# Weight conversion from float64: the sign by a Prelu on ScalarE in place of a GpSimd operation

## The chip, the cores and the metric

The kernel runs on one core of a Trainium2 chip, as one program. The metric is the time of one execution on the device in microseconds. Engines are called by name: TensorE (PE in rows; PEld is its weight load), VectorE (DVE), ScalarE (ACT), GpSimd (POOL) and SyncE (SP), which issues the DMAs.

## The reference

Windowed attention on 4 x 8 heads of 576 tokens (four heads with a window of 32, four with a dilated one), then two feed-forward layers on the 2304 tokens. Cut to its core:

```python
attn = softmax(where(mask, q @ k.T / 8, -1e9)) @ v
x = attn_out.transpose(0, 2, 1, 3).reshape(2304, 512)
xn = x / sqrt(mean(x * x) + 1e-6) * rms_g
y = (silu(xn @ w_gate) * (xn @ w_val)) @ w_out            # 512 -> 1536 -> 512
h = y @ w_in                                              # 512 -> 1024
solu = h * softmax(h)
out = (solu - mean(solu)) / sqrt(var(solu) + 1e-6) * g_ln @ w_out2
```

The weight matrices arrive as float64, since the scales that they were multiplied by are float64; q, k, v and the gains are float32.

## The kernel before

**Data.** Every product of a weight is made of three matmuls: the operand and the weight are each split into a high part, rounded to TensorE's float32 format, and the low rest (mm3, lines 607 to 609). The weights come in 52 tiles of 128x512 float64: 36 for the first layer (w1: 12 slices f of the hidden width, each with a tile for gate, value and output) and 16 for the second.

**Conversion.** `prepare` makes each float64 tile into float32 by integer work on its two 32-bit words. A DMA brings the raw tile (`fetch`). `shifted` (line 264) multiplies the high word, read as a float32, by 2^-112 on ScalarE, which moves the exponent's offset from float64's to float32's; the result is tile tf. `signs` (line 272) multiplies the high word by zero on GpSimd, which leaves a zero with the weight's sign in tile wf. `parts` (line 277) shifts the low word right by 29 and ORs it into wf on VectorE. `joined` (line 282) shifts tf left by 3, which drops its sign, and ORs it into wf on VectorE. `scaled` multiplies 8 of the tiles by the gain. `halves` (ScalarE) writes the high part h_w into the raw tile's buffer, and `lows` writes the rest, on GpSimd or VectorE. wf has 4 slots; a tile's slot is free again after its `lows`.

**Stages.** Attention for tokens 0 to 511 comes first, in pieces of 256 tokens, each followed by its root mean square (`rms`: squares, a matmul with ones, `eps`, `root` as a power on GpSimd, `diag` on VectorE, `spread` on TensorE, then scaling, high and low parts of x). The first layer runs over f for a piece of tokens: gate (g), value (vp), tanh, two products on VectorE, high and low parts (uh), output (y). Attention for the later pieces is laid between these products. The 36 tiles of w1 are converted while the first pieces run; the 16 tiles of the second layer are fetched into the buffers of w1 as the last piece lets go of them. The second layer then runs over 18 blocks of 128 tokens (`p_h`, `p_t`, `p_products`).

**Order.** All steps up to the second layer are written to the engines' queues in an order that a planner in the kernel works out (`Plan.order`). Each step has its engine or engines with a cost in us, the steps that it needs, the slots that it takes and a due time. At each turn the engine whose first step can start earliest takes, among the steps that could start within 0.25 us of that, the one with the lowest due time. A step with two engines goes to the one on which it ends first. The due times of w1's tiles are 14 + 2.72 us for each; those of the first attention groups rise by 2.5 us each. While TensorE would idle in the plan before the first `spread`, small dummy matmuls (warm) are written. The queues run in order on the chip, each instruction when its semaphores allow.

Of the kernel before, what the change touches and what calls it, by code (L numbers as in the profile page):

```python
# [7 lines left out]
F32 = mybir.dt.float32  # L8
# [3 lines left out]
U32 = mybir.dt.uint32  # L12
AF = mybir.ActivationFunctionType
ALU = mybir.AluOpType
# [6 lines left out]
P = 128  # L21
# [175 lines left out]
def tile_attention_glu_solu(ctx: ExitStack, tc: tile.TileContext, qk_d, v_d, w1_d, win2_d, wout2_d,  # L197
                            rmsg_d, gln_d, mask_d, ident_d, out):
    nc = tc.nc
    ENG = {"a": nc.scalar, "d": nc.vector, "p": nc.gpsimd}  # L200
    const = ctx.enter_context(tc.tile_pool(name="const", bufs=1))
    wp = ctx.enter_context(tc.tile_pool(name="wp", bufs=1))
    stg = ctx.enter_context(tc.tile_pool(name="stg", bufs=1))
# [24 lines left out]
    plan = Plan({"qk": 2, "v": 2, "a": 2, "y0": 1, "y1": 1, "y2": 1, "y3": 1, "g": 1, "vp": 1, "s": 3, "pT": 2, "x": 1,  # L228
                 "sq": 2, "rs": 1, "u": 2, "uh": 2, "yo": 2, "wf": 4, "bh": 1, "bl": 1, "ch": 1, "cl": 1,
                 "yl": 3, "yh": 3} | {f"w{f}_{i}": 1 for f in range(NF1) for i in range(3)})  # L230
    T = {}

    def new(pool_, key, shape, dtype=F32, name=None):

        tag, i = plan.where[key]
        T[key] = pool_.tile(shape, dtype, tag=f"{tag}{i}", name=name or tag)
        return T[key]

    def put(e, dst, src, scale=None):
        if e == "a":  # L240
            nc.scalar.copy(dst, src) if scale is None else nc.scalar.mul(dst, src, scale)  # L241
        elif e == "p":
            nc.gpsimd.tensor_scalar(dst, src, 1.0 if scale is None else scale, 1.0, ALU.mult, ALU.mult)
        elif scale is None:
            nc.vector.tensor_copy(dst, src)  # L245
        else:
            nc.vector.tensor_scalar(dst, src, scale, None, ALU.mult)

    def less(e, dst, a, b):
        ENG[e].tensor_tensor(dst, a, b, ALU.subtract)  # L250
# [5 lines left out]
    def prepare(key, tag, src, scale, due, needs=()):  # L256
        k, raw, tf, wf, th = ((x, key) for x in ("k", "raw", "tf", "wf", "th"))

        def fetch(e):
            r = T[raw] = wp.tile([P, 512, 2], I32, tag=tag, name=f"raw_{tag}")  # L260
            nc.sync.dma_start(out=r.rearrange("p n t -> p (n t)"), in_=src.bitcast(I32))

        def shifted(e):
            put(e, new(stg, tf, [P, 512], name="tf"), T[raw][:, :, 1].bitcast(F32), 2.0 ** -112)

        def wf_():
            return T["wf", key[0]][:, plan.where[wf][1]]

        def signs(e):
            if ("wf", key[0]) not in T:  # L270
                T["wf", key[0]] = xn.tile([P, 4, 512], F32, tag="cl0", name="wf")
            ENG[e].tensor_scalar(wf_(), T[raw][:, :, 1].bitcast(F32), 0.0, 1.0, ALU.mult, ALU.mult)  # L272

        def parts(e):

            w = wf_().bitcast(U32)
            nc.vector.scalar_tensor_tensor(out=w, in0=T[raw][:, :, 0].bitcast(U32), scalar=29, in1=w,
                                           op0=ALU.logical_shift_right, op1=ALU.bitwise_or)

        def joined(e):  # L280
            w = wf_().bitcast(U32)
            nc.vector.scalar_tensor_tensor(out=w, in0=T[tf].bitcast(U32), scalar=3, in1=w,
                                           op0=ALU.logical_shift_left, op1=ALU.bitwise_or)

        def scaled(e):
            put(e, wf_(), wf_(), scale)

        def halves(e):

            T[th] = wp.tile([P, 2, 512], F32R, tag=tag, name=f"h_{tag}")  # L290
            put(e, T[th][:, 0], wf_())

        def lows(e):
            less(e, T[th][:, 1], wf_(), T[th][:, 0])
            (w1 if key[0] == 1 else w2)[key[1:]] = T[th]

        plan.add((key, "fetch"), {"s": 1.6}, fetch, needs, due=due - 12)
        plan.add((key, "shifted"), {"a": 0.68}, shifted, [(key, "fetch")], takes=[("yo", tf)], due=due)
        lead = (key[0],) + ((0, 0) if key[0] == 1 else (0,))
        plan.add((key, "signs"), {"p": 1.0}, signs, [(key, "fetch")] + [(lead, "signs")] * (key != lead),  # L300
                 takes=[("wf", wf)] + [("cl", ("stage", key[0]))] * (key == lead), uses=[("stage", key[0])], due=due)
        plan.add((key, "parts"), {"d": 0.72}, parts, [(key, "signs")], due=due)
        plan.add((key, "joined"), {"d": 0.72}, joined, [(key, "parts"), (key, "shifted")], uses=[tf], due=due)
        before = "joined"
        if scale is not None:
            plan.add((key, "scaled"), {"d": 0.45, "p": 0.92}, scaled, [(key, "joined")], due=due)
            before = "scaled"
        plan.add((key, "halves"), {"a": 0.62}, halves, [(key, before)], due=due)
        plan.add((key, "lows"), {"p": 1.6, "d": 1.0}, lows, [(key, "halves")], uses=[wf, ("stage", key[0])], due=due)
# [499 lines left out]
    for name, t, src in (("mask", masks_t, mask_d), ("ident", ident, ident_d), ("rmsg", rmsg, rmsg_d), ("gln", gln, gln_d)):  # L809
        plan.add((name,), {"s": 0.5 if name in ("mask", "ident") else 0.1},  # L810
                 lambda e, t=t, src=src: nc.sync.dma_start(out=t, in_=src),
                 due={"mask": -9, "ident": -5.5}.get(name, 3))
# [8 lines left out]
    for f in range(NF1):  # L821
        for i in range(3):
            prepare((1, f, i), f"w{f}_{i}", w1_d[f, :, i * 512:(i + 1) * 512], None, 14 + 2.72 * (3 * f + i))
# [5 lines left out]
    for u in range(16):  # L829
        f, i = u // 3, u % 3  # L830
        src = win2_d[u // 2, :, (u % 2) * 512:(u % 2 + 1) * 512] if u < 8 else wout2_d[u - 8]
        prepare((2, u), f"w{f}_{i}", src, None if u < 8 else gln[:, u - 8:u - 7], 5000 + u,
                [("out", last, f, 1) if i == 2 else (("g", "vp")[i], last, f, 1)] + ([("gln",)] if u >= 8 else []))
# [130 lines left out]
```

## Time and profile before

| what | us |
|---|---|
| median of 3 runs | 790.29 |
| lowest to highest | 788.03 to 791.84 |
| the profiled execution, its own time | 789.12 |
| span of its instructions | 787.3 |
| TensorE busy | 762.3 |
| VectorE busy | 442.3 |
| ScalarE busy | 315.5 |
| GpSimd busy | 162.0 |

The span goes from the first instruction to the last. A busy time is the time in which at least one instruction of the engine ran; matmuls overlap, so a busy TensorE isn't TensorE at its peak. In rows, L272 is line 272 of the kernel, and a tile is named by the kernel's names, out<-in.

### The profile page before, as it was taken

The page shows a single profiled execution, that of the slowest core. Times are in us where ns is not written, and L with a number is a line of the kernel's source. Part 1 is how long each engine was busy: PE and PEld are TensorE (multiplying, and loading weights), DVE is VectorE, ACT ScalarE, POOL GpSimd, SP SyncE. Part 2 cuts the span into 40 slices and gives each one's busy share as a digit, 9 for nine tenths or more (in the row PEclk, how much of TensorE's full clock was granted, in tenths as well). Part 3 has the DMA queues.
Part 4 walks back from the last instruction along what each step waited for, and adds up shares of the span by engine and source line. Part 5 has one row for each costly group of instructions (what it writes and reads, how often), then busy time and mean ns, then how long its engine had stood idle before and what let it go on. Part 6 is the DMA issues. An engine that isn't in the chain of part 4 may idle for free. (4 is left out here: it accounts for less than half of the span.)

```text
span 787.3 us, 12213 instructions
## 1 busy us (share of the span) xinstructions
PE 762.3 (97%) x4776; PEld 627.9 (80%) x4776; DVE 442.3 (56%) x835; ACT 315.5 (40%) x780; POOL 162.0 (21%) x206
## 2 busy tenths in 40 slices
PE   8779999899999999999999999989999999999997
PEld 6668777689997787887788888768878888888886
DVE  4889999965444344434354438982255544444542
ACT  3555666644333333324333325431134434434432
POOL 1333544521120120210110304530011101101100
PEclk9999999999999999999999999999999999999999
DMA  7997111033014101033211027500101111111101
GB/s 258 359 409 297 56 39 72 25 127 124 14 28 137 65 32 48 1 104 120 76 36 49 1 97 235 163 27 1 63 4 54 50 32 54 42 40 54 35 33 41
DMA packets 34233, 68.94 MB, mean 88 GB/s; under 512 B 3328, under 2 KB 13568, under 8 KB 34176
## 3 DMA queue, kind: packets, MB, share of 16 engines
q1 hardware_dynamic: 34176, 68.16, 25.5%
q8 instruction: 38, 0.62, 0.3%
q14 instruction: 19, 0.16, 0.1%
HBM read 58.71 MB, written 9.44 MB: 87 GB/s over the span
## 5 line engine op out<-in xcount | busy, mean ns | idle before, releaser
L607 PE MATMUL y<-uh,h_w 128*128 128x512 f32 (+1 forms) x252 | 93.9, 372 | 1.3 <-ACT uh L241 0.9
L608 PE MATMUL y<-uh,h_w 128*128 128x512 f32 (+1 forms) x252 | 91.0, 361 | 0.8 <-DVE uh L250 0.8
L609 PE MATMUL y<-uh,h_w 128*128 128x512 f32 (+1 forms) x252 | 90.9, 361 | 0.4 <-DVE h_w L250 0.4
L643 DVE SCALAR_TENSOR_TENSOR u<-u,g 128x512 f32<-128x512 f32 (+1 forms) x63 | 38.3, 608 | 87.3 <-ACT u L637 86.9
L607 PE MATMUL vp<-xh,h_w 128*128 128x512 f32 (+1 forms) x204 | 81.4, 399 | 0.6 <-DVE u L647 0.6
L607 PE MATMUL g<-xh,h_w 128*128 128x512 f32 (+1 forms) x204 | 79.8, 391 | 2.1 <-DVE u L643 2.0
L609 PE MATMUL vp<-xh,h_w 128*128 128x512 f32 (+1 forms) x204 | 77.6, 380 | 0.9 <-POOL h_w L250 0.9
L608 PE MATMUL g<-xl,h_w 128*128 128x512 f32 (+1 forms) x204 | 77.5, 380 | 0.8 <-POOL xl L250 0.5
L609 PE MATMUL g<-xh,h_w 128*128 128x512 f32 (+1 forms) x204 | 77.5, 380 | 0.1
L608 PE MATMUL vp<-xl,h_w 128*128 128x512 f32 (+1 forms) x204 | 77.4, 379 | 0.0
L637 ACT ACTIVATE u<-g 128x512 f32<-128x512 f32 (+1 forms) x63 | 33.6, 534 | 79.6 <-PE g L609 79.2
L272 POOL TENSOR_SCALAR wf<-raw_w 128x512 f32<-128x512 f32 x52 | 46.1, 888 | 93.8 <-DVE h_w L250 44.7
L503 POOL TENSOR_TENSOR sq<-x 128x256 f32<-128x256 f32 x30 | 20.0, 669 | 219.5 <-DVE x L245 179.3
L241 ACT CAST uh<-u 128x512 fp32r<-128x512 f32 (+1 forms) x63 | 35.2, 558 | 74.0 <-DVE u L647 74.0
L647 DVE SCALAR_TENSOR_TENSOR u<-u,vp 128x512 f32<-128x512 f32 (+1 forms) x63 | 38.3, 608 | 43.4 <-PE vp L609 43.2
L762 POOL TENSOR_SCALAR st<-st 128x1 f32<-128x1 f32 x18 | 13.5, 748 | 222.8 <-ACT sq L760 222.8
L384 ACT ACTIVATE s<-s,nm 128x64 f32<-128x64 f32 x120 | 40.3, 337 | 45.9 <-DVE nm L370 45.9
L746 PE MATMUL h<-h_w,yh 128*128 128x512 f32 x144 | 58.2, 404 | 0.0
L787 PE MATMUL o<-h_w,lt 128*128 128x512 f32 (+1 forms) x152 | 57.9, 381 | 0.2 <-DVE lt L775 0.2
L785 PE MATMUL o<-h_w,lt 128*128 128x512 f32 (+1 forms) x152 | 57.7, 380 | 0.0
L786 PE MATMUL o<-h_w,lt 128*128 128x512 f32 (+1 forms) x152 | 57.6, 379 | 0.0
L748 PE MATMUL h<-h_w,yh 128*128 128x512 f32 x144 | 57.0, 396 | 0.0
(116 smaller groups left out, 1663.5 us busy)
## 6 DMA issues: line engine op xcount, KB each, us to landing
raw_w<-w SPq DMA_DIRECT2D x36, 512.0 KB, 10.2
vt<-v SPq DMA_DIRECT2D x38, 256.0 KB, 3.0
qk<-qk SPq DMA_DIRECT2D x20, 400.0 KB, 4.0
y<-yT SPq DMA_DIRECT2D x18, 256.0 KB, 3.1
yT<-yo SPq DMA_DIRECT2D x16, 256.0 KB, 2.3
raw_w<-win SPq DMA_DIRECT2D x8, 512.0 KB, 4.6
raw_w<-wout SPq DMA_DIRECT2D x8, 512.0 KB, 4.2
out<-ob SPq DMA_DIRECT2D x16, 256.0 KB, 2.1
```

The lines of the kernel that those rows point to most:

```text
L272: ENG[e].tensor_scalar(wf_(), T[raw][:, :, 1].bitcast(F32), 0.0, 1.0, ALU.mult, ALU.mult)
L384: nc.scalar.activation(T[s_][:, i], (T[sp] if first else T[s_])[:, i], AF.Exp, scale=0.125 if first else 1.0, bias=st["nm"][:, i:i + 1], a ...
L607: nc.tensor.matmul(acc, wh, xh, start=first, stop=False)
L608: nc.tensor.matmul(acc, wh, xl, start=False, stop=False)
L609: nc.tensor.matmul(acc, wl, xh, start=False, stop=last)
L643: return lambda e: nc.vector.scalar_tensor_tensor(out=u_of(f), in0=u_of(f), scalar=1.0, in1=T["g", v, f], op0=ALU.add, op1=ALU.mult)
L647: return lambda e: nc.vector.scalar_tensor_tensor(out=u_of(f), in0=u_of(f), scalar=0.5, in1=T["vp", v, f], op0=ALU.mult, op1=ALU.mult)
L746: nc.tensor.matmul(h[:, n], yh[:, 0, k], w[:, 0], start=(k == 0), stop=False)
L748: nc.tensor.matmul(h[:, n], yh[:, 1, k], w[:, 0], start=False, stop=(k == KD - 1))
L785: nc.tensor.matmul(o, lt[:, 0, k], w[:, 0], start=(k == 0), stop=False)
L786: nc.tensor.matmul(o, lt[:, 0, k], w[:, 1], start=False, stop=False)
L787: nc.tensor.matmul(o, lt[:, 1, k], w[:, 0], start=False, stop=(k == NF2 - 1))
```

## The change

The Prelu in `shifted` scales by 2^-112 and multiplies negative results by -2^32. A negative weight's tf is thus positive and has one exponent bit set that no other weight sets; the shift left by 3 in `joined` moves that bit into the sign's place. `signs` and its step are gone. `parts` writes wf where it had ORed into it, as a one-source shift; it needs only the fetch (and the first tile's `parts`, where it had been the first tile's `signs`), takes the wf slot, and has a cost of 0.42 in the plan where it had 0.72.

```diff
--- before.py
+++ after.py
@@ -261,21 +261,19 @@
             nc.sync.dma_start(out=r.rearrange("p n t -> p (n t)"), in_=src.bitcast(I32))
 
         def shifted(e):
-            put(e, new(stg, tf, [P, 512], name="tf"), T[raw][:, :, 1].bitcast(F32), 2.0 ** -112)
+
+
+            nc.scalar.activation(new(stg, tf, [P, 512], name="tf"), T[raw][:, :, 1].bitcast(F32), AF.Prelu,
+                                 scale=2.0 ** -112, alpha=-2.0 ** 32)
 
         def wf_():
             return T["wf", key[0]][:, plan.where[wf][1]]
 
-        def signs(e):
+        def parts(e):
+
             if ("wf", key[0]) not in T:
                 T["wf", key[0]] = xn.tile([P, 4, 512], F32, tag="cl0", name="wf")
-            ENG[e].tensor_scalar(wf_(), T[raw][:, :, 1].bitcast(F32), 0.0, 1.0, ALU.mult, ALU.mult)
-
-        def parts(e):
-
-            w = wf_().bitcast(U32)
-            nc.vector.scalar_tensor_tensor(out=w, in0=T[raw][:, :, 0].bitcast(U32), scalar=29, in1=w,
-                                           op0=ALU.logical_shift_right, op1=ALU.bitwise_or)
+            nc.vector.tensor_scalar(wf_().bitcast(U32), T[raw][:, :, 0].bitcast(U32), 29, None, ALU.logical_shift_right)
 
         def joined(e):
             w = wf_().bitcast(U32)
@@ -297,9 +295,8 @@
         plan.add((key, "fetch"), {"s": 1.6}, fetch, needs, due=due - 12)
         plan.add((key, "shifted"), {"a": 0.68}, shifted, [(key, "fetch")], takes=[("yo", tf)], due=due)
         lead = (key[0],) + ((0, 0) if key[0] == 1 else (0,))
-        plan.add((key, "signs"), {"p": 1.0}, signs, [(key, "fetch")] + [(lead, "signs")] * (key != lead),
+        plan.add((key, "parts"), {"d": 0.42}, parts, [(key, "fetch")] + [(lead, "parts")] * (key != lead),
                  takes=[("wf", wf)] + [("cl", ("stage", key[0]))] * (key == lead), uses=[("stage", key[0])], due=due)
-        plan.add((key, "parts"), {"d": 0.72}, parts, [(key, "signs")], due=due)
         plan.add((key, "joined"), {"d": 0.72}, joined, [(key, "parts"), (key, "shifted")], uses=[tf], due=due)
         before = "joined"
         if scale is not None:
```

## Rows read from the trace of the kernel before

**Rows 1.** The page, part 1: busy us, share of the span, instructions.

```profile
PE 762.3 (97%) x4776; PEld 627.9 (80%) x4776; DVE 442.3 (56%) x835; ACT 315.5 (40%) x780; POOL 162.0 (21%) x206
```

**Rows 2.** Table by stretches: the stretch, its length, each engine's busy us, TensorE's clock, DMA.

```profile
30.00:70.00 40.00, 32.17 (x278) 28.76 (x277) 36.85 (x76) 20.25 (x50) 12.39 (x15) 0.96 1.03 407
70.00:150.00 80.00, 78.64 (x509) 63.04 (x509) 76.46 (x128) 50.04 (x126) 36.56 (x38) 1.00 0.17 58
150.00:160.00 10.00, 7.80 (x74) 5.48 (x72) 9.79 (x17) 5.68 (x17) 6.05 (x7) 1.00 0.39 136
...
500.00:540.00 40.00, 37.79 (x162) 29.69 (x161) 30.44 (x42) 15.34 (x27) 12.88 (x11) 1.00 0.17 54
```

**Rows 3.** Waits of TensorE, 28 to 70 us: us, times, longest.

```profile
PE pv L419 <- DVE x L245: 2.2, 1, 2.2
PE rs L536 <- DVE rd L533: 1.6, 2, 0.8
PE vp L609 <- POOL h_w L250: 0.9, 1, 0.9
```

**Rows 4.** Waits of TensorE, 70 to 165 us.

```profile
PE tp L402 <- DVE s L396: 1.4, 2, 0.7
PE tp L402 <- DVE x L245: 1.1, 1, 1.1
```

**Rows 5.** Groups by line and shape: count | busy us, mean ns | idle us before.

```profile
L272 POOL TENSOR_SCALAR wf<-raw_w 128x512 f32<-128x512 f32 x52 | 46.1, 888 | 93.8 <-DVE h_w L250 44.7 <-DMA raw_w<-win 26.9 <-DMA raw_w<-w 18.1
...
L241 ACT ACTIVATE tf<-raw_w 128x512 f32<-128x512 f32 x52 | 34.6, 671 | 10.8 <-DVE wf L282 4.7 <-DMA raw_w<-win 3.6 <-DMA raw_w<-w 1.5
...
L637 ACT ACTIVATE u<-g 128x512 f32<-128x512 f32 x45 | 26.8, 595 | 70.8 <-PE g L609 70.8
...
L760 ACT ACTIVATE sq<-e,st 128x1024 f32<-128x1024 f32 x18 | 20.7, 1151 | 35.0 <-DVE st L758 35.0
...
L250 POOL TENSOR_TENSOR h_w<-wf,h_w 128x512 fp32r<-128x512 f32 x14 | 19.1, 1363 | 24.1 <-ACT h_w L241 18.7 <-issue 5.4
...
L247 DVE TENSOR_SCALAR wf<-wf,gln 128x512 f32<-128x512 f32 x4 | 1.9, 483 | 0.1
...
L854 ACT ACT_TABLE_LOAD x1 | 1.3, 1283 | 0.7 <-PEq L957 0.7
```

**Rows 6.** Tile raw_w: ns min/median/max, first and last start in us.

```profile
L272 POOL TENSOR_SCALAR wf<-raw_w x52: 635/974/1181, 12.4 to 517.8; 128x512 f32<-128x512 f32 x52
...
L277 DVE SCALAR_TENSOR_TENSOR wf<-raw_w,wf x52: 674/684/1784, 21.0 to 521.9; 128x512 uint32<-128x512 uint32 x52
```

**Rows 7.** Order of time, GpSimd: start us, us, instruction.

```profile
26.70 1.10 POOL L272 TENSOR_SCALAR wf<-raw_w 128x512 f32<-128x512 f32 x1 [4.49 <-DMA raw_w<-w]
27.77 0.72 POOL L528 TENSOR_TENSOR r<-r,mhalf 128x2 f32<-128x2 f32 x1
...
61.27 1.28 POOL L250 TENSOR_TENSOR h_w<-wf,h_w 128x512 fp32r<-128x512 f32 x1 [1.36 <-ACT h_w L241]
```

**Rows 8.** Order of time, VectorE.

```profile
28.52 0.48 DVE L533 TENSOR_SCALAR rd<-ident,r 128x128 f32<-128x128 f32 x2 [1.24 <-POOL r L528]
...
61.84 1.26 DVE L282 SCALAR_TENSOR_TENSOR wf<-tf,wf 128x512 uint32<-128x512 uint32 x1
```

**Rows 9.** Line 277 (parts) by stretches: VectorE's busy us and count.

```profile
30.00:70.00 40.00, 7.38 (x11) 0.96 1.03 407
70.00:160.00 90.00, 19.90 (x25) 1.00 0.19 67
```

**Rows 10.** Line 272 (signs) by stretches: GpSimd's busy us and count.

```profile
30.00:70.00 40.00, 6.57 (x9) 0.96 1.03 407
70.00:160.00 90.00, 19.87 (x22) 1.00 0.19 67
460.00:540.00 80.00, 15.49 (x16) 1.00 0.40 129
```

**Rows 11.** Waits over the whole span: us, times, longest.

```profile
POOL wf L272 <- DMA raw_w<-w: 18.1, 4, 11.1
```

## Prediction

> **What bounds the kernel now.** I read the busy times first [rows 1]: TensorE is busy for 762.3 of 787.3 us, so all that an edit on the other engines can win is TensorE's 25 us of idle time and whatever makes its own work run late or slowly. The next view is the table by stretches [rows 2], because the average hides where the idle time lies. In 30 to 70 us TensorE is busy for 32.17 of 40 us, and VectorE for 36.85: 7.8 us of TensorE are lost while VectorE is nearly full. In 70 to 150 us TensorE loses 1.4 us and in 150 to 160 us 2.2 us, with VectorE at 76.46 of 80 and 9.79 of 10. In 500 to 540 us it loses 2.2 us, with VectorE at 30.44 of 40. These are just the stretches in which weights are converted: 36 tiles up to 160 us, 16 tiles after 467 us. The waits of TensorE say what ended its idle time there: VectorE's copy into x (2.2 us) and VectorE's diagonal rd (1.6 us) early [rows 3], VectorE's s and x after 70 us [rows 4]. So weight conversion competes with attention and the gated products for VectorE, and VectorE's queue is what TensorE waits for. GpSimd has time left, but it isn't innocent, as the next part shows.
>
> **What goes away: 52 sign operations on GpSimd.** They take 888 ns each, 46.1 us in all [rows 5]; the shortest takes 635 ns [rows 6]. The difference is a collision. In one place GpSimd works on a low half from 61.27 to 62.55 us, and a joining instruction on VectorE that starts at 61.84 us takes 1.26 us [rows 7, 8], where the parts instruction of the same size has a median of 684 ns [rows 6]: it ends about 0.6 us late, roughly what GpSimd still had to do when it began. Seen from GpSimd, the sign operations lose 6.57 - 9 x 0.635 = 0.9 us in 30 to 70 us, 19.87 - 22 x 0.635 = 5.9 us in 70 to 160 us and 15.49 - 16 x 0.635 = 5.3 us in 460 to 540 us [rows 6, 10]. I take as much for what VectorE loses to them, as an estimate: a collision holds up one side or the other. The Trainium skill says the same under GPSIMD Engine Reference, Specifications: GpSimd's SBUF interfaces are shared with VectorE, and it contends with instructions of VectorE that read two SBUF operands or run in a 2-port mode; by that rule the new, one-source parts instruction would still collide with whatever GpSimd work is left, so that the collisions would shrink and not vanish. The trace agrees with the first half; no row of it shows a one-source conversion step beside GpSimd.
>
> A second cost goes with them. GpSimd takes its work in order, and at 26.70 us a sign operation, having waited 4.49 us for its DMA, runs until 27.80 us; the power for the first tile's mean square can start only at 27.77 us, and VectorE's rd idles 1.24 us for it [rows 7, 8]. That chain leads through TensorE's spread and the scaling of x to the first gate matmul, and nothing hides it.
>
> **What is changed on VectorE.** Parts becomes a one-source shift in place of a two-source shift and OR. The nearest row below is the one-source multiplication of a 128x512 tile in SBUF, 483 ns [rows 5]; the nearest above is the parts instruction as it is, 684 ns [rows 6]. I take 483 ns, since it has the same number of operands and the same size. What speaks for the upper end is that the source is read at every second word, but the old parts instruction read it so too. The saving is then 0.20 us a tile; at the upper end it is 0.
>
> **What is changed on ScalarE.** The scaled copy (671 ns) becomes a Prelu with the same source, scale and destination [rows 5]. No row has a Prelu. Nearest below is the tanh of 128x512, 595 ns; the next function above is the square of twice the size, 1151 ns [rows 5]. I take 671 ns, since scaled copy, tanh and square run at nearly the same pace. The bounds are -52 x 0.08 = -4 us and 52 x 0.48 = 25 us of ScalarE's time. It is spread over stretches in which ScalarE is busy for half of the time (20.25 of 40 us, 50.04 of 80 us) [rows 2], and that idle time hides it: I take 0. If the cover were gone at the upper end, 36 x 0.48 = 17 us would fall into the first conversion, with some 50 us of idle time against it, so I leave it out of the range.
>
> **What is moved.** Parts now waits for the DMA itself, where the sign operation had waited (18.1 us in all, four times, for the first weights [rows 11]). Behind it in VectorE's queue stand attention, the norm and the gated products. It costs nothing as long as parts comes up after the landing: the first sign operation starts at 12.4 us, the first parts at 21.0 us [rows 6], and the order is by due time, which the change leaves alone. Behind GpSimd's missing instruction come the power, the squares, the low halves of x and 14 of the 52 low halves of weights; all move up. ScalarE's and SP's steps keep their needs; no DMA is added. The planner lays out the whole order anew with parts at 0.42 for 0.72 and GpSimd free, so single instructions will stand elsewhere.
>
> **The sum.** VectorE is relieved by 11 x 0.20 + 0.9 = 3.1 us in 30 to 70 us and by 25 x 0.20 + 5.9 = 10.9 us in 70 to 160 us [rows 9, 10], and by 16 x 0.20 + 5.3 = 8.5 us in the second conversion. Not all of it is time:
> - up to 30 us: the power comes about 1.2 us earlier, which is on the path: -1.2 us.
> - 30 to 70 us: 3.8 us of the waits are put down to VectorE in [rows 3] alone, 7.8 us are idle, so most of the 3.1 us can be won. I take 70%: -2.2 us.
> - 70 to 160 us: 10.9 us of relief meet 3.6 us of idle TensorE; beyond that TensorE is the limit. I take 40% of the idle time, since part of it ends with ScalarE's or TensorE's own chain: -1.4 us.
> - 500 to 540 us: 2.2 us idle, but there parts follows the landing closely and may wait for it: -0.2 us.
>
> Together -5.0 us. The profiled execution took 789.1 us (span 787.3 us and 1.8 us around it), which makes 784.1 us; it lay 1.2 us under the median of 790.3 us, so the forecast is 785.3 us. The bounds: with no saving on parts and only the earlier power, -1 us; with all idle time of the three stretches and the power won, -(1.2 + 7.8 + 3.6 + 2.2) = -15 us, which I don't believe, as TensorE also waits for DMA and for its own results.
>
> **The rivals.**
> 1. Hidden: TensorE gets its operands no earlier because its own order and ScalarE's chain come last. For it: TensorE is busy for 78.64 of 80 us in the longest conversion stretch. Against: the 7.8 us lost in 30 to 70 us. Time: 789 to 790 us.
> 2. Low halves go to GpSimd (the other side). The planner gives each of the 52 low halves to whichever of VectorE and GpSimd ends first; with GpSimd free, more than the present 14 may go there, at 1363 ns each [rows 5] against 684 ns on VectorE for work of that size [rows 6]. TensorE then waits for them: 0.9 us, the one time it shows [rows 3]. The gain of 5.0 us is eaten by six such waits, and at ten the kernel is 4 us slower: 794 us. Against it: 14 such steps now cause one such wait, so ten would need some 140.
> 3. VectorE blocks on landings: parts planned ahead of the data stops everything behind it. If the 18.1 us of GpSimd's DMA waits [rows 11] fell on VectorE, less the first, in which VectorE has nothing to do anyway (11.1 us), it would be 7 us: 790.3 - 5.0 + 7 = 792 us. Against: the 9 us between the first sign operation and the first parts.
> 4. The change doesn't do what it says: Prelu lies outside the loaded function table. Only one table load stands in the trace, 1283 ns [rows 5], and it serves the exponential, tanh, square and copies. If Prelu needed its own, each of 52 would bring two loads, 104 x 1.28 = 133 us on ScalarE, half of it hidden at best: 857 us or more. The Trainium skill has the rule under ScalarE: Activation LUTs, Table sets: functions are loaded in named sets, a function outside the active set needs a load, and cheap functions such as relu and copy are in every set. By that rule the question is whether Prelu counts as such a filler; no row of this trace shows a Prelu.
>
> **How the numbers follow.** The forecast (781 to 788.5 us as its own range) has a chance of 0.58, rival 1 0.22, rival 2 0.10, rival 3 0.07, rival 4 0.03. A change of 0.5%, 3.95 us, is about what the measurement of this kernel can tell from none: faster means under 786.3 us, slower over 794.2 us. Of the forecast 0.50 lies under 786.3 us and 0.08 above; rival 1 gives 0.02 to faster and 0.20 to same; rival 2 splits in halves, rival 3 gives 0.04 to slower, rival 4 all. Faster 0.52, same 0.36, slower 0.12. The range of 8 in 10 leaves out the far end of rivals 2 to 4 and gains above 10.5 us: 779.8 to 791.8 us.
>
> **What would show it.** GpSimd's busy time falls by about 46 us, unless low halves fill it; parts shows a median near 483 ns; Prelu near 671 ns with one table load in all; rd waits less than 0.3 us for the power and the first gate matmul starts about 1.2 us earlier; TensorE is busy for over 34 us of the 40 that follow 30 us. I'm wrong if TensorE's idle time in 30 to 70 us stays near 7.8 us, if its waits for low halves from GpSimd grow to several us, or if VectorE's parts waits for raw weights.

## The result and the profile after

| what | before | after |
|---|---|---|
| median, us | 790.61 | 781.59 |
| lowest to highest | 788.03 to 791.84 | 779.74 to 783.07 |
| the profiled execution, its own time | 789.12 | 782.46 |
| span of its instructions | 787.3 | 780.7 |

The ratio after to before is 0.9889, with a 95% interval of 0.9854 to 0.9923: 9.0 us less, where 5.0 us had been forecast. The profiled executions differ by 6.7 us alone; before's was 1.5 us under its median, and after's 0.9 us over.

The page of the changed kernel, part 1 (as [rows 1]), and its table by stretches (as [rows 2]):

```profile
PE 763.8 (98%) x4775; PEld 634.7 (81%) x4775; DVE 416.3 (53%) x838; ACT 315.8 (40%) x781; POOL 111.2 (14%) x150
```

```profile
30.00:70.00 40.00, 35.57 (x277) 33.09 (x276) 31.79 (x76) 21.83 (x54) 5.99 (x7) 0.79 0.98 381
70.00:150.00 80.00, 78.53 (x551) 64.44 (x550) 75.12 (x140) 54.45 (x140) 23.37 (x22) 1.00 0.23 80
150.00:160.00 10.00, 10.00 (x71) 7.67 (x70) 3.93 (x9) 2.42 (x7) 2.36 (x4) 1.00 0.38 122
500.00:540.00 40.00, 40.00 (x178) 33.12 (x177) 22.98 (x38) 13.30 (x23) 2.64 (x2) 1.00 0.13 41
```

GpSimd loses 50.8 us of work and VectorE 26.0. The numbers in brackets are counts of instructions, and where the same kind of work runs they say more than TensorE's busy time. In 30 to 70 us TensorE is 3.4 us busier than before, yet ran 277 matmuls where it had run 278: its granted clock was 0.79 there where it had been 0.96. In 70 to 160 us it ran 620 where it had run 581 (the rows count a matmul that crosses their border twice); of these 39, 20 only make up for work that came later (up to 70 us it had run 570 where it had run 590), and the stretch mixes short matmuls of attention with longer ones, so that its count alone doesn't size the gain. In 500 to 540 us all matmuls are of one size. There it ran 178 where it had run 162, and the stretch ahead shows that 178 is what 40 us hold when nothing is late (table by stretches, before):

```profile
460.00:500.00 40.00, 40.00 (x178) 33.12 (x177) 29.32 (x38) 17.12 (x29) 14.18 (x14) 1.00 0.63 203
```

Groups by line and shape, after (as [rows 5]); then tile raw_w (as [rows 6]):

```profile
L280 DVE SCALAR_TENSOR_TENSOR wf<-tf,wf 128x512 uint32<-128x512 uint32 x52 | 37.2, 717 | 3.7 <-ACT tf L266 0.6 <-DVE wf L276 0.5
L266 ACT ACTIVATE tf<-raw_w 128x512 f32<-128x512 f32 x52 | 34.6, 674 | 9.7 <-DMA raw_w<-win 4.7 <-DMA raw_w<-wout 2.6 <-DMA raw_w<-w 2.3
...
L276 DVE TENSOR_SCALAR wf<-raw_w 128x512 uint32<-128x512 uint32 x52 | 25.5, 493 | 1.9 <-DMA raw_w<-win 1.9
```

```profile
L276 DVE TENSOR_SCALAR wf<-raw_w x52: 415/421/1514, 21.2 to 514.4; 128x512 uint32<-128x512 uint32 x52
```

Parts has a median of 421 ns (before 684). The joining step, whose instruction is unchanged, has a mean of 717 ns where it had 862 (the same group of before), which the experiments below put down to GpSimd being out of its way.

Where the 6.6 us of span lie is read from the starts of four kinds of instruction in order of time: the first gate matmul, the first gate matmul of the last pieces (g<-xhl), the first fetch of the second layer's weights (it stands on SP, and waits for buffers to come free), and the first matmul of the second layer. Before:

```profile
31.14 0.39 PE L607 MATMUL g<-xh,h_w 128*128 128x256 f32 x1
...
165.05 0.28 PE L607 MATMUL g<-xhl,h_w 128*128 128x256 f32 x1
...
467.28 3.04 SPq L261 DMA_DIRECT2D raw_w<-win  x2
...
565.94 0.39 PE L746 MATMUL h<-h_w,yh 128*128 128x512 f32 x1
```

After:

```profile
33.50 0.39 PE L604 MATMUL g<-xh,h_w 128*128 128x256 f32 x1
...
163.21 0.28 PE L604 MATMUL g<-xhl,h_w 128*128 128x256 f32 x1
...
464.30 3.03 SPq L261 DMA_DIRECT2D raw_w<-win  x2
...
559.29 0.39 PE L743 MATMUL h<-h_w,yh 128*128 128x512 f32 x1
```

| stage | before, us | after, us | change | forecast |
|---|---|---|---|---|
| to the first gate matmul | 31.14 | 33.50 | +2.4 | -1.2 |
| to g<-xhl (36 tiles converted) | 133.91 | 129.71 | -4.2 | -3.6 |
| to the second layer's first fetch | 302.23 | 301.09 | -1.1 | 0 |
| to the second layer (16 tiles converted) | 98.66 | 94.99 | -3.7 | -0.2 |
| second layer | 221.4 | 221.4 | 0 | 0 |

### The profile page after: what moved, and what is told of

The parts are those of the page before. It is cut to its first block, busy times and chain, and to the rows that moved or that the text cites. A ratio compares the mean times of both kernels' runs of the same rounds, so it can differ in the third digit from the quotient of the medians.

```text
span 780.7 us, 12092 instructions
## 1 busy us (share of the span) xinstructions
PE 763.8 (98%) x4775; PEld 634.7 (81%) x4775; DVE 416.3 (53%) x838; ACT 315.8 (40%) x781; POOL 111.2 (14%) x150
## 4 chain that ended last, share of the span: by engine, by line
PE 89%; DVE 5%; DMA 2%; issue 1%; ACT 1%; POOL 1%; SPq 0%; ACTq 0%; POOLq 0%; DVEq 0%
PE vp L604 7%; PE y L604 6%; PE vp L606 6%; PE vp L605 6%; PE g L604 6%; PE y L605 6%; PE g L606 6%; PE y L606 6%; PE g L605 6%; PE h L745 4%; PE h L743 4%; PE h L744 4%; PE o L784 4%; PE o L783 4%; PE o L782 4%; PE pv L416 3%
## 5 line engine op out<-in xcount | busy, mean ns | idle before, releaser
L743 PE MATMUL h<-h_w,yh 128*128 128x512 f32 x144 | 58.2, 404 | 0.0
L745 PE MATMUL h<-h_w,yh 128*128 128x512 f32 x144 | 57.0, 396 | 0.0
L744 PE MATMUL h<-h_w,yh 128*128 128x512 f32 x144 | 56.8, 395 | 0.0
L604 PEld LDWEIGHTS y<-uh,h_w 128*128 128x128 f32 x252 | 48.0, 191 | 9.1 <-ACT uh L241 1.2
```

The lines of the kernel that those rows point to most:

```text
L604: nc.tensor.matmul(acc, wh, xh, start=first, stop=False)
L743: nc.tensor.matmul(h[:, n], yh[:, 0, k], w[:, 0], start=(k == 0), stop=False)
L744: nc.tensor.matmul(h[:, n], yh[:, 0, k], w[:, 1], start=False, stop=False)
L745: nc.tensor.matmul(h[:, n], yh[:, 1, k], w[:, 0], start=False, stop=(k == KD - 1))
```

## The experiments

Three theories stood against each other. A: the time comes from the operations, that is from VectorE's shorter step and from the collisions that leave with GpSimd's sign operations. B: it comes from the order, which the planner lays out anew with GpSimd free and parts at 0.42. C: it is made or lost ahead of the first gate matmul, and the rest only keeps that lead. Each experiment is an edit of the changed kernel; ratios are to the kernel before, measured beside it on the same chip. None leaves anything out of the computation; e2, e7 and e8 add work on GpSimd whose result nobody reads.

### The changed kernel again, and the new operations in the old order

e0 is the changed kernel. In e1 the planner sees the old steps, so that the work is laid out as before, but the step of the sign operation emits nothing:

```diff
-        plan.add((key, "parts"), {"d": 0.42}, parts, [(key, "fetch")] + [(lead, "parts")] * (key != lead),
+        plan.add((key, "signs"), {"p": 1.0}, lambda e: None, [(key, "fetch")] + [(lead, "signs")] * (key != lead),
...
+        plan.add((key, "parts"), {"d": 0.72}, parts, [(key, "signs")], due=due)
```

> The changed kernel once more, beside the experiments, as their common measure. Theory A (the operations themselves: less GpSimd work that collides with VectorE, a shorter parts) and theory B (the planner's new order) both expect 780 to 783 us against 790.6 us before. By its profile the TensorE clock stood at half speed from 26.5 to 29.9 us and from 36.7 to 53.8 us; if that belongs to this order and is no accident, it shows again here.

> The new operations in the order of the kernel before: the planner still counts a step of 1.0 us on GpSimd and 0.72 us for parts, but the GpSimd step writes no instruction. Queues of TensorE, ScalarE and SP are those of the kernel before, VectorE's differs only in the form of parts. Theory A: all of the gain, 781 to 783 us. Theory B: none of it, 789 to 791 us. A share in between splits the gain between the two.

e0 took 780.57 us, ratio 0.9849 (0.9818 to 0.9881), with 792.77 us before beside it: 12.2 us. e1 took 784.35 us, ratio 0.9894 (0.9858 to 0.993): 8.4 us of the 12.2 are there without the new order. Neither theory had this: A expected 781 to 783 us and B 789 to 791. The two intervals overlap, so that the order's 3.8 us are a difference of medians, and the profiles show little of it: from the first gate matmul to g<-xhl e1 takes 130.2 us, where e0 takes 128.9 and the result's profile 129.7, and the later stages agree to 0.2 us.

### The old operations in the new order

e6 is the other corner: the scaled copy (not shown in the cut), GpSimd's sign operation (emitted inside parts) and the two-source parts, in the plan of the changed kernel.

```diff
...
-            nc.vector.tensor_scalar(wf_().bitcast(U32), T[raw][:, :, 0].bitcast(U32), 29, None, ALU.logical_shift_right)
+            w = wf_().bitcast(U32)
+            nc.gpsimd.tensor_scalar(wf_(), T[raw][:, :, 1].bitcast(F32), 0.0, 1.0, ALU.mult, ALU.mult)
+            nc.vector.scalar_tensor_tensor(out=w, in0=T[raw][:, :, 0].bitcast(U32), scalar=29, in1=w,
+                                           op0=ALU.logical_shift_right, op1=ALU.bitwise_or)
```

> The three old operations (scaled copy, sign on GpSimd, two-source parts that waits for it) in the order of the changed kernel. With the GpSimd work back this order took 791 us, with the two-source parts 785 us, the changed kernel 781 us. Theory A (operations; their costs add up): 793 to 797 us, slower than the kernel before by 1 to 4 us, since this order counts on a short parts and an idle GpSimd. Theory B (the new order is better by itself by some 4 us, as the run with the old order suggests): 787 to 789 us.

It took 808.45 us, ratio 1.0217 (1.0183 to 1.025) to 792.96 us: 15.5 us slower than before, and outside what either theory gave. Waits of VectorE (30 to 165 us) and of TensorE (70 to 165 us) in e6:

```profile
DVE wf L277 <- POOL wf L276: 7.7, 8, 1.8
```

```profile
PE tp L401 <- DVE s L395: 9.3, 5, 3.2
```

The new order puts parts where no sign operation has to be waited for. With one there, VectorE stops for 7.7 us in its queue, and TensorE behind it for 9.3 us. So B falls as a cause by itself: the same order loses 15.5 us with the old operations, while with the new ones its median lies 3.8 us lower. The four corners do not add up, and neither does an account that prices operations and order apart.

### GpSimd's work back, and cut in two

e2 puts a GpSimd operation of nearly the old size back beside each parts, into a tile that nobody reads (`spare`). VectorE doesn't wait for it. But it reads the raw tile, into which `halves` writes, so `halves` waits for it. e8 keeps that wait and takes away the work (one column is read). e7 adds the work back, reading a constant in place of the raw tile.

```diff
 e2:
+            nc.gpsimd.tensor_scalar(spare, T[raw][:, 0:480, 1].bitcast(F32), 0.0, 1.0, ALU.mult, ALU.mult)
 e8:
+            nc.gpsimd.tensor_scalar(spare[:, 0:1], T[raw][:, 0:1, 1].bitcast(F32), 0.0, 1.0, ALU.mult, ALU.mult)
 e7: as e8, and
+            nc.gpsimd.tensor_scalar(spare, mhalf[:, 0:1].to_broadcast([P, 480]), 0.0, 1.0, ALU.mult, ALU.mult)
```

> The changed kernel in its own order, with 52 sign operations back on GpSimd, on 480 of 512 columns, into a spare tile that nobody reads; halves must wait for them before it overwrites the raw tile. Theory A with the collisions as its larger part: 4 to 6 us slower than the changed kernel, 786 to 788 us, with joined and the low halves back near 860 and 760 ns in the mean. Theory A with parts as its larger part, and theory B: within 1 us of the changed kernel.

> The changed kernel in its own order with GpSimd kept as busy as by the sign operations, but with nothing of weight waiting for it: for each tile a one-column read of the raw tile, and then 480 columns read from a constant and written to a spare tile. Theory A with the collisions as the cause: as slow as with the sign operations back, 788 to 792 us. Rival: the cost lay in what waited for the sign operation (halves, which overwrites the raw tile): 780 to 783 us.

> The same with the one-column read alone: the wait of halves for GpSimd is there, GpSimd's long work is not. Theory A with the collisions as the cause: within 2 us of the changed kernel, 780 to 783 us. Rival (the wait): as slow as with the sign operations back, 788 to 792 us.

| kernel | median, us | ratio to before, interval |
|---|---|---|
| e2, work and wait | 791.35 | 0.9996 (0.9968 to 1.0024) |
| e7, work apart and wait | 787.19 | 0.9926 (0.9895 to 0.9958) |
| e8, wait alone | 782.17 | 0.9846 (0.9814 to 0.9878) |
| e0, neither | 780.57 | 0.9849 (0.9818 to 0.9881) |

Groups by line and shape, e2:

```profile
L282 DVE SCALAR_TENSOR_TENSOR wf<-tf,wf 128x512 uint32<-128x512 uint32 x52 | 42.0, 809 | 3.2 <-ACT tf L267 0.3
L277 POOL TENSOR_SCALAR spare<-raw_w 128x480 bf16<-128x480 f32 x52 | 41.4, 797 | 38.3 <-DMA raw_w<-win 31.8 <-DMA raw_w<-wout 4.7
...
L642 DVE SCALAR_TENSOR_TENSOR u<-u,g 128x512 f32<-128x512 f32 x45 | 30.8, 684 | 78.8 <-ACT u L636 78.8
...
L278 DVE TENSOR_SCALAR wf<-raw_w 128x512 uint32<-128x512 uint32 x52 | 28.5, 550 | 1.4 <-DMA raw_w<-win 1.4
```

The same view, e7 and then e8:

```profile
L283 DVE SCALAR_TENSOR_TENSOR wf<-tf,wf 128x512 uint32<-128x512 uint32 x52 | 40.7, 784 | 3.7 <-ACT tf L267 0.6 <-ACT h_w L242 0.5
L278 POOL TENSOR_SCALAR spare<-mhalf 128x480 bf16<-128x480 f32 x52 | 39.7, 763 | 4.3
```

```profile
L282 DVE SCALAR_TENSOR_TENSOR wf<-tf,wf 128x512 uint32<-128x512 uint32 x52 | 37.8, 728 | 3.3 <-ACT tf L267 0.5
...
L277 POOL TENSOR_SCALAR spare<-raw_w 128x1 bf16<-128x1 f32 x52 | 18.7, 359 | 48.3 <-DMA raw_w<-win 35.8 <-DMA raw_w<-wout 10.8
```

Waits of ScalarE's `halves` for the GpSimd operation over the whole span, e7 and then e8:

```profile
ACT h_w L242 <- POOL spare L277: 9.4, 9, 2.5
```

```profile
ACT h_w L242 <- POOL spare L277: 6.1, 4, 2.1
```

e2 gives back all that the change had won: with the shorter parts, the Prelu and the new order in place, 52 unread operations on GpSimd cost 10.8 us. It is not the wait that costs: in e8 ScalarE waits 6.1 us for the short operations, which add 18.7 us to GpSimd's work, and the kernel is as fast as e0, while the same view of e2 has no such wait at all. It is the work on many elements: with it the unchanged joining step takes 809 ns (e2) and 784 ns (e7), without it 728 (e8) and 717 (the changed kernel). The work that e7 adds to e8 shares no tile with VectorE's conversion, so a shared tile isn't needed for the collision.

The traces show the collision directly, instruction by instruction. In the 14 profiles of this case VectorE runs 1409 two-source steps of 128x512 with both operands in SBUF (parts as it was, joined, low halves) while no GpSimd instruction runs, and each takes 675 to 696 ns. Another 674 run beside GpSimd, and 377 of these take over 700 ns, up to 1789. The two products with g and vp, whose second operand lies in PSUM, take 668 to 689 ns beside GpSimd too, all 189 of them; in e2 they keep their 684 ns in the mean, where joined has 809.

Neither e2 nor e7 came in where it was expected: e2's 791.35 us lie above the 786 to 788 of theory A with the collisions as its larger part, e7's 787.19 under its 788 to 792. The share of collisions that e7 bears out is 787.19 - 782.17 = 5.0 us, of which the 3.3 us more that `halves` waits may be a part. The further 4.2 us of e2, whose operation reads the raw tile, go with VectorE's busy time: 416.2 us in e0 and e8, 426.1 in e7, 430.7 in e2 (whose profiled execution was the longest of its twelve). Why reading the raw tile holds VectorE up more stays open.

### VectorE's parts as two-source again

In e3 parts keeps its place, but ORs with a column of zeros, which is set once at the start (not shown), so that it reads two operands.

```diff
-            nc.vector.tensor_scalar(wf_().bitcast(U32), T[raw][:, :, 0].bitcast(U32), 29, None, ALU.logical_shift_right)
+            nc.vector.scalar_tensor_tensor(out=wf_().bitcast(U32), in0=T[raw][:, :, 0].bitcast(U32), scalar=29,
+                                           in1=zeros.to_broadcast([P, 512]), op0=ALU.logical_shift_right, op1=ALU.bitwise_or)
```

> The changed kernel in its own order, with parts as a two-source instruction again (shift and OR with a column of zeros): 684 ns for 493 ns, 10 us of VectorE in all, nothing else changed. Theory A with parts as its larger part: 3 to 5 us slower than the changed kernel, 784 to 787 us. Theory A with the collisions as its larger part: 1 to 2 us slower. Theory B: within 1 us.

It took 784.55 us, ratio 0.9891 (0.9858 to 0.9925): 4.0 us over e0 in medians, with intervals that overlap. Groups by line, e3:

```profile
L277 DVE SCALAR_TENSOR_TENSOR wf<-raw_w,zeros 128x512 uint32<-128x512 uint32 x52 | 39.3, 756 | 1.9 <-DMA raw_w<-win 1.9
```

Parts grows from 25.5 to 39.3 us of VectorE's time, and 4.0 of these 13.8 us arrive in the time. So both halves of A are there. Which is the larger isn't settled: put back by itself, GpSimd's work costs 5.0 us (e7) to 10.8 (e2) and the two-source parts 4.0, and e3 fell where parts as the larger half had been expected. The shares don't add up to the whole either (10.8 and 4.0 against 12.2).

### One layer's conversion alone

e4 has the new operations and steps for the first layer's 36 tiles only, e5 for the second layer's 16 only; the others keep the old ones. Shown are the steps of the plan.

```diff
+        if key[0] == 1:      # e5: == 2
             plan.add((key, "parts"), {"d": 0.42}, parts, [(key, "fetch")] + [(lead, "parts")] * (key != lead),
...
+        else:
+            plan.add((key, "signs"), {"p": 1.0}, signs, [(key, "fetch")] + [(lead, "signs")] * (key != lead),
...
+            plan.add((key, "parts"), {"d": 0.72}, parts, [(key, "signs")], due=due)
```

> The change made for the 36 tiles of the first layer alone; the 16 tiles of the second are converted as before. By the traces of the changed kernel the first layer's share is 2.8 us of 6.7 us within the span, measured at the same matmul before and after: about 787 to 789 us where the changed kernel has 781 and the kernel before 791 to 793. The prediction's own split (4.8 of 5.0 us in the first conversion) expects nearly all of the gain here, 781 to 783 us.

> The change made for the 16 tiles of the second layer alone. By the traces its share is 3.7 us: 787 to 789 us, with no wait of TensorE left in 500 to 540 us, where the kernel before lost 2.2 us. The prediction's own split gave it 0.2 us: 790 to 793 us.

Beside 792.49 us before, e4 took 782.68 us (ratio 0.9875, 0.9843 to 0.9908) and e5 788.96 us (0.9946, 0.9918 to 0.9974): -9.8 and -3.5 us, together 13.3 where e0 has 12.2. e4 came in where the prediction's split had it (781 to 783 us) and not where the profiles had (787 to 789), e5 (787 to 789 by the profiles, 790 to 793 by the prediction) the other way round. Table by stretches, 500 to 540 us, e4 and then e5:

```profile
500.00:540.00 40.00, 37.58 (x161) 29.86 (x162) 28.33 (x40) 14.30 (x25) 12.88 (x11) 1.00 0.12 41
```

```profile
500.00:540.00 40.00, 40.00 (x178) 33.10 (x178) 28.67 (x47) 16.59 (x29) 4.92 (x4) 1.00 0.24 81
```

With the old second conversion TensorE runs 161 matmuls in this stretch, with the new one 178. The second conversion's gain is thus confined to its stretch, and the timed 3.5 us agree with the stage's 3.7.

e5 also gives a fairer pair for the first conversion. It has before's operations there, and its first gate matmul starts as late as e0's. First gate matmul and first g<-xhl, e5 and then e0:

```profile
34.88 0.38 PE L622 MATMUL g<-xh,h_w 128*128 128x256 f32 x1
...
171.02 0.28 PE L622 MATMUL g<-xhl,h_w 128*128 128x256 f32 x1
```

```profile
34.79 0.38 PE L604 MATMUL g<-xh,h_w 128*128 128x256 f32 x1
...
163.72 0.28 PE L604 MATMUL g<-xhl,h_w 128*128 128x256 f32 x1
```

From equal starts, and at a mean granted clock of 0.83 up to 70 us in both, the new conversion arrives 7.3 us earlier. The 4.2 us of the table above are less, and the clock is the likely reason: before's profiled execution ran 30 to 70 us at a mean granted clock of 0.96 and after's at 0.79, and with the same conversion e5 (0.83) takes 136.1 us for the stage where before took 133.9.

The pair also says where they are won. The sixth gate product (the 41st g<-xh matmul) starts just behind 70 us, e5 and then e0:

```profile
72.48 0.28 PE L622 MATMUL g<-xh,h_w 128*128 128x256 f32 x1
```

```profile
71.90 0.28 PE L604 MATMUL g<-xh,h_w 128*128 128x256 f32 x1
```

Counted from the first gate matmul e0 is 0.5 us ahead here (1.8 us at the end of the product before, with a piece of attention in between). From here to g<-xhl e5 takes 98.5 us, of which TensorE is idle for 4.2, and e0 takes 91.8, idle for 1.5: 6.7 us are won where the idle time fell by 2.8.

### The start, and the steps behind it

The changed kernel's one visible loss is the first gate matmul, 2.4 us later than before. e10 lets the fetches of all weights but the first slice's wait for the queries and keys on SP's queue. e11 gives the copies into x for tokens 256 to 511, for one of which TensorE waits 2.2 us, to ScalarE. e9 keeps all low halves of weights on VectorE (rival 2 turned round).

```diff
 e10 (in the call of prepare for the first layer):
-            None, 14 + 2.72 * (3 * f + i))
+            None, 14 + 2.72 * (3 * f + i), [("load_qk", (1, 3))] if f else [])
 e11 (the engines of copy):
-            {"a": 0.5, "d": 0.45} if first else {"d": 0.5}, copy,
+            {"a": 0.5} if t == 1 else {"a": 0.5, "d": 0.45} if first else {"d": 0.5}, copy,
 e9 (the engines of lows):
-            {"p": 1.6, "d": 1.0}
+            {"d": 1.0}
```

> The changed kernel with the raw tiles from the fourth on fetched only after the last queries and keys of the first 512 tokens; the queues of TensorE, VectorE, ScalarE and GpSimd are unchanged, SP's alone differs. In the changed kernel TensorE waits 1.6 to 2.4 us for a load of queries and keys between 22 and 25 us, and its clock is at half speed for 14 to 24 us before 54 us. Theory C (the late load and the low clock take part of the gain back): the wait shrinks, the first gate matmul starts 1 to 2 us earlier, and the kernel takes 776 to 780 us. Rival: VectorE is the limit up to 160 us, so an earlier start and a higher clock are lost again: 780 to 783 us. If the raw tiles come too late for parts, it is slower.

> The changed kernel with the four copies of attention results into x for tokens 256 to 511 fixed to ScalarE; the planner lays the order out anew. In every run so far TensorE waits 2.2 us near 36 us for such a copy on VectorE, with a stretch of 3 to 14 us at half clock right behind. Theory C (this wait and the low clock behind it still cost time): the wait goes, less time at half clock, 776 to 779 us. Rival (VectorE's total work up to 160 us sets the time, and the order is as good or as bad as any other): 779 to 783 us.

> The changed kernel with all 52 low halves on VectorE; the planner lays the order out anew. 12 low halves on GpSimd cost 17 us of GpSimd at 1.4 us each; on VectorE they cost 12 x 0.69 = 8 us, while VectorE loses about 10 us less to collisions with GpSimd in the two conversions. Theory A: within 3 us of the changed kernel, 778 to 784 us. Rival 2 of the prediction (TensorE waits for low halves on GpSimd): 3 us or more faster, under 778 us.

e10 took 780.96 us (ratio 0.9862, 0.982 to 0.9904), e11 781.01 (0.9854, 0.9824 to 0.9884), e9 781.40 (0.9863, 0.9826 to 0.9901): none differs measurably from the changed kernel's 0.9849. In e10's profiled execution the first gate matmul starts at 29.93 us and the span is 776.9 us, so a lead of the start is kept to the end there. But e8, with the changed kernel's order on SP, has 30.10 us and 777.4 us too, and with the old first conversion e5 has 34.88 us and e6 29.50. The start varies between executions of either kind, and C doesn't explain the difference between the kernels. Nor does the low clock: in 40 to 50 us it is between 0.50 and 0.58 in 12 of the 14 profiles, those of e5 and e6 among them; only before (1.00) and e1 (0.84) lie higher. In e11 the wait only changes its name, from VectorE (2.2 us) to ScalarE (1.7 us).

In e9 GpSimd has 18 us less to do and VectorE twelve low halves more, and nothing comes of it: where the few low halves lie makes no difference that can be measured. No run was measurably faster than the changed kernel.

## Why the prediction was right in direction and half in size

**What bounds the kernel: right.** TensorE is the bound, VectorE's queue is what it waits for where weights are converted, and the relief reaches TensorE only there.

**What goes away: right.** The forecast took 0.9 + 5.9 + 5.3 us of collisions from GpSimd's side [rows 6, 10]. With the 0.20 us a tile, VectorE's relief came to 22.5 us; its busy time fell by 26.0. Of these 52 x 0.263 = 13.7 us are parts' own, and the other 12.3 are near the 12.1 taken for the collisions. That VectorE loses as much as GpSimd was an assumption that no run tests by itself, so the close agreement may be luck. GpSimd's busy time fell by 50.8 us (46 forecast). e2, e7 and e8 show the collisions as a cause, at 5.0 to 10.8 us of run time.

**VectorE's new step: its saving under-sized.** I took 483 ns with bounds up to 684 and none below; the median is 421 ns, 0.26 us under the old one for 0.20. "Nothing below" was not justified: the row I leaned on multiplies, and no row showed a shift with one source.

**ScalarE's new step: right.** The Prelu takes 674 ns against 671 of the scaled copy, and one table load stands in the trace, so rival 4 is out (groups by line, after):

```profile
L851 ACT ACT_TABLE_LOAD x1 | 1.3, 1283 | 0.7 <-PEq L954 0.7
```

**What is moved: right.** The low halves on GpSimd went from 14 to 12, not up, so rival 2 is out. Rival 3's wait, which I had named as a sign of being wrong, is there, but small (waits over the whole span, after):

```profile
DVE wf L276 <- DMA raw_w<-win: 1.9, 2, 1.6
```

**The term up to 30 us, -1.2: the wait is gone, and the start is no earlier.** The first rd no longer waits for the power, which now waits for VectorE; I had asked for under 0.3 us. Order of time, GpSimd and VectorE, after:

```profile
29.21 0.83 POOL L525 TENSOR_TENSOR r<-r,mhalf 128x2 f32<-128x2 f32 x1 [8.36 <-DVE r L522]
30.07 0.48 DVE L530 TENSOR_SCALAR rd<-ident,r 128x128 f32<-128x128 f32 x2
```

But the term rested on one execution. e5 has the sign operation in the same place, and there it ended 2.15 us before the power could start (order of time, GpSimd, e5):

```profile
28.32 0.64 POOL L278 TENSOR_SCALAR wf<-raw_w 128x512 f32<-128x512 f32 x1 [5.73 <-DMA raw_w<-w]
...
31.11 0.83 POOL L543 TENSOR_TENSOR r<-r,mhalf 128x2 f32<-128x2 f32 x1 [2.15 <-DVE r L540]
```

So whether the sign operation delays the power depends on whether its tile lands before the mean square is there. I had also written that nothing hides this delay, but part of it is hidden: from VectorE's r, the step ahead of the power, to rd it takes 2.3 us before and 1.1 after, and to the first gate matmul 4.95 and 4.53. And TensorE had been late already, for the queries and keys; order of time, before and then after:

```profile
23.22 0.69 PE L355 MATMUL sp<-qk 128*64 128x64 f32 x16 [0.80 <-DMA qk<-qk]
```

```profile
25.00 0.69 PE L352 MATMUL sp<-qk 128*64 128x64 f32 x16 [2.42 <-DMA qk<-qk]
```

These matmuls start 1.8 us later, by more than the term was worth. I had taken before's start as fixed, when the first gate matmul starts anywhere from 29.50 to 34.88 us in the profiles of all runs.

**The term for 30 to 70 us, -2.2: not shown by its own sign.** I wanted TensorE busy for over 34 us of 40. It was, at 35.57 us, but for another reason: 277 matmuls for 278, with TensorE's granted clock at 1.2 GHz for part of the time. The finer table by stretches of after has it:

```profile
35.00:40.00 5.00, 2.83 (x25) 2.72 (x25) 4.36 (x12) 2.41 (x11) 1.52 (x2) 0.67 0.74 267
40.00:45.00 5.00, 5.00 (x36) 4.87 (x35) 2.92 (x8) 1.64 (x4) 0.00 (x1) 0.50 1.01 370
45.00:50.00 5.00, 4.41 (x34) 4.21 (x32) 3.46 (x8) 3.61 (x9) 0.00 (x0) 0.50 1.01 410
```

The same table of before:

```profile
40.00:45.00 5.00, 3.94 (x47) 3.47 (x42) 3.59 (x8) 3.84 (x10) 0.69 (x1) 1.00 1.02 412
45.00:50.00 5.00, 3.92 (x27) 3.29 (x26) 4.39 (x10) 2.41 (x5) 2.56 (x4) 1.00 1.03 411
```

After, TensorE was busy for 2.83 of 5 us, and then for 9.41 of 10 us at half the clock, in which it ran 68 matmuls; before, it ran 71 in 7.86 us at the full clock. A low clock fills the busy column, so the column can't serve as a sign of gain. The waits of TensorE, 28 to 70 us after, say what was won of [rows 3]: rd's 1.6 us are gone and the low halves' 0.9 are 0.3, while x's 2.2 us stand as they were.

```profile
PE pv L416 <- DVE x L245: 2.2, 1, 2.2
...
PE g L606 <- POOL h_w L250: 0.3, 1, 0.3
```

From equal starts the gain up to the sixth gate product is 0.5 us, 1.8 at most (e5 and e0 above), so this term was if anything too large.

The clock goes with the spread of the times: among executions of before one at a mean granted clock of 0.997 took 788.01 us and one at 0.982 took 797.16.

**The terms for 70 to 160 us and 500 to 540 us, -1.4 and -0.2: the step that failed.** I set what could be won by TensorE's idle time, 3.6 and 2.2 us ("beyond that TensorE is the limit"), and then took a share. In the first stretch the change won 6.7 us where the idle time fell by 2.8 (e5 and e0 above). In the second, 16 matmuls were missing; at 40 / 178 = 0.225 us each that is 3.6 us, and the change won 3.7, again more than the idle time. The idle time is too small a cap, because a matmul's row lasts longer than its turn. Two steps of before, in order of time:

```profile
510.48 0.39 PE L608 MATMUL y<-uh,h_w 128*128 128x512 f32 x1
510.71 0.39 PE L609 MATMUL y<-uh,h_w 128*128 128x512 f32 x1
511.26 0.50 PE L607 MATMUL g<-xh,h_w 128*128 128x512 f32 x1 [0.16 <-DVE u L643]
511.60 0.40 PE L608 MATMUL g<-xl,h_w 128*128 128x512 f32 x1
```

Undisturbed, one starts every 0.23 us and its row lasts 0.39. From 510.71 to 511.60 us two turns take 0.89 us where 0.45 would do: 0.44 us are lost, and the row reports 0.16 us of idle time. The Trainium skill gives the general form, under Perfetto Trace Analysis, Identifying the Most-Contended Engine: matmul busy time is no good measure of how near TensorE is to its limit, since matmuls are pipelined, and the busy share of the weight loads is one to use instead. The trace agrees: PEld had 29.69 us in the stretch from 500 to 540 us [rows 2] where it now has 33.12. That column stood in my own rows, and it would have sized the last term. For 70 to 160 us no undisturbed stretch with the same mix of matmuls is there to compare with.

My reason for the small share of the last term fell too. Parts does follow the landings there (1.9 us of waits), but TensorE has work in hand for so long: none of its waits is left in 500 to 540 us in e5 or in the changed kernel.

**Between the conversions, 0: -1.1 us.** Nothing ties this to the change: over the 14 profiles the stage takes 301.1 to 302.2 us, with the old operations (e6 301.09) as with the new (e10 302.02).

**Rival 1 (hidden)** had 789 to 790 us, and the kernel takes 781.59; its argument was the same busy column, 78.64 of 80 us.

**The total.** The relief of VectorE was sized well; what TensorE makes of it was not. Of the four terms one rested on a single execution, one was too large and two were too small, so that the sum of 5.0 us owes its nearness to 9.0 (12.2 in e0) in part to errors that offset each other.

## What to carry to other kernels

Size what TensorE can win in a stretch by its count of matmuls against a stretch with the same work that runs undisturbed, or by its weight loads, not by its idle time; and look at the granted clock before a fuller busy column is called a gain. Work on GpSimd that nobody waits for isn't free: price it by what VectorE's instructions take beside it. Where a planner lays out the queues, an operation and the order made for it are one change, and taking one of them alone can cost more than both win.

## What was not expected of the hardware

VectorE's two-source steps of 128x512 with both operands in SBUF take 675 to 696 ns, without exception in 1409 cases, while GpSimd runs nothing, and up to 1789 ns beside it; the same size of step with one operand in PSUM stays at 668 to 689 ns beside GpSimd.

The one-source shift of a 128x512 tile of 32-bit words, read at every second word, takes 421 ns in the median, less than the 483 ns of the one-source multiplication in [rows 5], and the two-source form 684 ns.

A one-source instruction of VectorE collides as well. Order of time, after, GpSimd and then VectorE:

```profile
505.74 1.58 POOL L250 TENSOR_TENSOR h_w<-wf,h_w 128x512 fp32r<-128x512 f32 x1 [0.74 <-DMA raw_w<-wout]
506.19 1.40 DVE L247 TENSOR_SCALAR wf<-wf,gln 128x512 f32<-128x512 f32 x1
```

The gain's multiplication takes 1.40 us beside GpSimd, where its mean had been 483 ns [rows 5], and ends shortly after GpSimd's instruction does. Parts itself collides too: 43 of its 52 instructions run clear of GpSimd and take at most 428 ns, and the nine that overlap with it take 838 ns in the mean, up to 1514. The Trainium skill, under GPSIMD Engine Reference, Specifications, names, besides instructions with two SBUF inputs, those that run in a 2-port mode. The trace now agrees that one-source ones are held up, and doesn't show the mode. In the prediction I had left this condition out where I concluded that the one-source parts would still collide; the conclusion came true.

An instruction of GpSimd on one column takes 359 ns, and 52 of them cost no time that could be measured (e8).
